# Fused attention and ELU feed-forward on one core: the largest magnitudes spread through PSUM instead of DRAM

## The chip, the cores and the metric

The kernel runs on one core of a Trainium2 chip. The core has a matrix engine (PE, with its weight loads shown apart as PEld), a vector engine (DVE), an activation engine (ACT), a general engine (POOL), and a sync engine whose queue (SP) issues all the kernel's DMA transfers, in order. SBUF is the on-chip memory with 128 partitions, PSUM the small memory that PE writes and DVE and ACT read, DRAM the memory outside. The metric is the device time of one execution in microseconds (us); lower is better.

## The reference, cut to what matters

```python
# q, k, v: (8 batches, 8 heads, 576 positions, 64), s: (8, 8, 576); all float32
scores = q @ k^T / 8, masked causally, plus min(-(cum_i - cum_j), 0)   # cum: running sum of max(s, 0)
attn   = softmax(scores)                    # row by row
x      = (attn @ v), heads side by side     # (4608 tokens, 512)
h      = x @ w_in                           # w_in (512, 2048)
g      = where(h > 0, h, exp(min(h, 0)) - 1)
out    = g @ w_out                          # w_out (2048, 512), float32
```

## The kernel before, in words

The attention runs by batch, by pair of heads (four pairs in a batch, `j`), and by blocks of 128 queries. The feed-forward part runs by chunks (`ch`, twelve of 384 tokens), and inside a chunk by 16 blocks of 128 hidden columns (`f`). For each `f`, PE makes the hidden product `h` (line 1312), ACT and DVE turn it into `gg` (lines 1276, 1321, 1330), and PE adds the projection to `o` (line 1349). Attention and feed-forward are interleaved. PE makes the scores `sc` (line 964), DVE adds the mask and takes the minimum (`p`, `mn`, line 967), ACT takes the exponential (line 972), POOL, ACT and DVE make halves of `p` (lines 1017, 1021, 1025), DMA transposes turn them (`T`, line 383), and PE weighs the values with them (`av`, line 1126).

Most products use two float16 halves of each operand, a high half and a low half, after scaling by a power of two. The scale comes from the largest magnitude of the operand, over all partitions. Chunk 0 is the exception: it runs in float32 (lines 1296 and 1341) while the scales of the weights aren't known yet. Attention of the first three batches' early blocks also runs in float32 and needs none.

The function `scales_of` finds such scales. It is called nine times: once for the two weight matrices (with three spans of columns), and once for each of eight groups of values. `peak` (line 574) has put one largest magnitude for each partition and each loaded piece into a column of `peaks`. `scales_of` reduces these to one number for each partition (`own`, line 593), stores them into DRAM (`aside`, 128 numbers of 4 bytes for each span), and loads the 128 numbers back into every partition (`every`). DVE then takes the largest in each partition and turns its exponent into a scale (lines 596, 598, 582). `split_unit` uses the weights' scales: it makes 32 high halves (line 402, 403) and 32 low halves on DVE (line 650) before chunk 1 can run. `group_values` loads the values of a group (`va`), takes their peaks and asks for their scale, 60 steps of priority ahead of their use.

The order of all instructions is set by a planner, `Plan.issue`. Each operation has a priority, a list of engines with assumed costs, and the buffers that it takes. The planner keeps a clock for each engine and always takes the operation that can start first, the priority deciding ties. For a transfer it assumes a lag until the data has landed: 5000 ns for the store to `aside`, 4500 ns for the load of `every`, 1800 ns for most others. Each engine then runs its list in the order found, and an instruction whose data isn't there holds up what stands behind it on the same engine. On SP this means that a load that waits holds up all later transfers. PSUM banks are buffers too: tag `a` (2 banks) and tag `av` (1 bank) serve scores, turned tiles and the weighing of values; tags `h` and `o0` to `o2` serve the feed-forward part, and scores when these are free.

Of the kernel before, what the change touches and what calls it, by code (L numbers as in the profile page):

```python
# [9 lines left out]
F32 = mybir.dt.float32  # L10
F32R = mybir.dt.float32r
U32 = mybir.dt.uint32
# [3 lines left out]
ALU = mybir.AluOpType  # L16

P = 128
# [6 lines left out]
SMALLEST = 2.0**-12  # L25
TOP, DOWN = 13, 22
# [55 lines left out]
class Plan:  # L82
# [87 lines left out]
    def issue(self):  # L170
# [3 lines left out]
        taken = dict.fromkeys(self.tags, 0)  # L174
# [15 lines left out]
        while pending:  # L190
            if free["PE"] > FILL_T:
                for o in [o for o in pending if o.filler]:
                    pending.remove(o)
                    for b in o.bufs:
                        b.users -= 1
                if not pending:
                    break
            best = None
            held = slots.get(self.signal, ())
            busy = free["PE"] > DYN_T or held and held[-1].users and not held[-1].others  # L200
            for o in pending:
                t = 0.0
                for b, k in o.new:
                    at = None
                    if taken[b.home] == k:
                        b.key, b.bufs = b.home, b.home_bufs
                        at = slot_free(b.key, b.bufs)
                    if b.others and (b.always or not busy):
                        for key, bufs, *rule in b.others:
                            if rule and not rule[0](taken[key]):  # L210
                                continue
                            other = slot_free(key, bufs)
                            if other is not None and (at is None or other < at):
# [26 lines left out]
            engine = self.ENGINE.get(engine, engine)  # L240
            if len(o.ways[n]) > 3:

                pipe = max(pipe, end) + o.ways[n][4] / RATE
                lag = pipe + o.ways[n][3] - end
            self.log.append((engine, start, end, o.prio))
            free[engine] = end
            for b, k in o.new:
                gone = skipped.setdefault(b.home, set())
                gone.add(k)
                while taken[b.home] in gone:  # L250
                    gone.remove(taken[b.home])
                    taken[b.home] += 1
                slots.setdefault(b.key, []).append(b)
            for b in o.bufs:
                b.until = max(b.until, end + lag)
                b.users -= 1
            pending.remove(o)
            for d in o.before:
                d.ready[engine] = max(d.ready.get(engine, 0.0), end + lag)
            for d in o.behind:  # L260
                d.ready[None] = max(d.ready.get(None, 0.0), start)
            for d in (*o.before, *o.behind):
                d.left -= 1
                if not d.left:
                    pending.append(d)
            at = len(block.instructions)
            trace()
            for i in block.instructions[at:]:
                if i.engine in last:
                    self.tc.add_manual_dep(  # L270
                        i, last[i.engine],
                        mybir.DependencyInfo(
                            mybir.DependencyClass.NoSync, mybir.DependencyReason.DATA
                        ),
                        reason="planned order",
                    )
                last[i.engine] = i.name
# [8 lines left out]
def pe4(n):  # L286

    return 4 * pe(n)
# [41 lines left out]
def kernel(  # L330
# [26 lines left out]
    D = vb.shape[4]  # L357
# [19 lines left out]
    def load(prio, dst, src, reads, writes, nbytes, late=(), lag=LAG):  # L377
        return op(prio, [("SP", SP_COST, lambda: nc.sync.dma_start(dst(), src()), lag, nbytes)],
                  reads, writes, late)
# [182 lines left out]
    A_GROUP = A_OUT + NF + 1  # L562
    peaks = plan.buf(const, [P, A_GROUP + len(groups) * (NP + 1)], F32, "peaks")

    scales = plan.buf(const, [P, 4 + 2 * len(groups)], F32, "scales")

    def scale_tiles():
        op(-8, [("Pool-M", 400.0, lambda: pool.memset(peaks.v, SMALLEST))], [], [peaks])
        op(-8, [("Pool-M", 60.0, lambda: pool.memset(scales.v, 1.0))], [], [scales])

    def peak(prio, n, src, reads, at, axis=mybir.AxisListType.X, aside=None, also=()):

# [8 lines left out]
    def power(out, src, top):  # L581
        dve.tensor_scalar(out, src, -1.0, float(top << 23), ALU.mult, ALU.add)

    def scales_of(prio, spans, dst):

        n = len(spans)
        own = plan.buf(sb, [P, n], F32, f"own_{dst}", tag=f"own{n}")
        aside = plan.buf(dram, [n, P], F32, f"aside_{dst}")
        every = plan.buf(sb, [P, n * P], F32, f"every_{dst}", tag=f"every{n}")

        def largest():
            for m, (at, k) in enumerate(spans):
                dve.tensor_reduce(own.v[:, m : m + 1], peaks.v[:, at : at + k], mybir.AxisListType.X, ALU.max)

        def exponents():
            dve.tensor_reduce(own.v, every.v.rearrange("p (n q) -> p n q", q=P), mybir.AxisListType.X, ALU.max)
            bits = own.v.bitcast(U32)
            dve.tensor_scalar(bits, bits, 23, 23, ALU.logical_shift_right, ALU.logical_shift_left)
            power(scales.v.bitcast(U32)[:, dst : dst + n], bits, 2 * 127 + TOP)

        used = [(peaks, m) for at, k in spans for m in range(at, at + k)]
        op(prio, [("DVE-SB", 60.0 + 70 * n, largest)], used, [own])
        load(prio, lambda: aside.v.rearrange("n p -> p n"), lambda: own.v, [own], [aside], P * n * 4, lag=5000.0)
        load(prio, lambda: every.v, lambda: aside.v.rearrange("n p -> (n p)").partition_broadcast(P),
             [aside], [every], P * P * n * 4, lag=4500.0)
        op(prio, [("DVE-SB", 500.0 + 130 * n, exponents)], [every], [own, (scales, dst)])

    def weight_scales():

# [213 lines left out]
    def group_values(u):  # L823

        at = groups.index((u.b, u.blocks[0] > 0))
        prio, first, col = u.prio - V_AHEAD, A_GROUP + at * (NP + 1), 4 + 2 * at
        home = w_parts[NG - 1] if at == 0 else w_all[(at - 1) % 2]
        va = plan.buf(sb, [P, NP, 2 * (NQ + 1), D], F32, f"va_{at}", tag=home.key[1])
        for j in range(NP):
            load(prio, lambda j=j: va.v[:, j], lambda j=j: vb[u.b, j, :, 1:], [], [(va, j)], P * 2 * (NQ + 1) * D * 4)  # L830
            peak(prio, 2 * (NQ + 1) * D, lambda j=j: va.v[:, j], [(va, j)], first + j, mybir.AxisListType.XY)
        scales_of(prio, [(first, NP + 1)], col)
        back = scales.v.bitcast(U32)
        op(prio, [("DVE-SB", 100.0, lambda: power(
            back[:, col + 1 : col + 2], back[:, col : col + 1], 2 * 127 - 15))], [(scales, col)], [(scales, col + 1)])
        return va, col
# [683 lines left out]
```

## Time and profile before

| what | value |
|---|---|
| median of 3 runs (lowest to highest) | 1129.79 us (1126.95 to 1129.88) |
| the profiled execution's own time | 1122.94 us |
| its span, first to last instruction | 1121.1 us |
| mean granted PE clock | 0.974 |
| DVE, ACT, POOL busy | 76%, 58%, 38% |
| DMA, mean rate | 140 GB/s |

The profile is of one execution, and its clock starts at the first instruction. A row of the order of time gives the start, the length (both in us), the engine, the source line, the operation, `out<-in`, and in brackets how long the engine had been idle before it, and what ended that idle time. SPq rows are the transfers' issues, not their landing. In a table by stretches, each engine has its busy time and its number of instructions; then follow the granted clock of PE (1.00 is full speed), the busy share of the DMA engines and their rate in GB/s. A row of waits gives the sum in us, the number of times and the longest.

### The profile page before, as it was taken

The numbers are of one execution on the slowest core, as the hardware profiler recorded it, in microseconds if no ns is written. First come the engines' busy times: TensorE is split into PE (matmuls) and PEld (weight loads), VectorE is DVE, ScalarE is ACT, GpSimd is POOL, SyncE is SP. The second block draws the span as 40 slices with busy tenths as digits, with TensorE's granted clock in tenths as the row PEclk, the third lists the DMA queues.
The fourth block names the chain that finished last, engine by engine and source line by source line (L and its number), as shares of the span: only waits on it lengthen the run. The fifth ranks groups of instructions, "written<-read, shape, count | busy, mean of one in ns | idle before, by whom it ended". The sixth has DMA issues, their size and how long they took to land. (4 is left out here: it accounts for less than half of the span.)

```text
span 1121.1 us, 19607 instructions
## 1 busy us (share of the span) xinstructions
PE 1036.3 (92%) x5970; PEld 614.3 (55%) x5970; DVE 856.2 (76%) x2218; ACT 646.5 (58%) x1525; POOL 422.4 (38%) x644
## 2 busy tenths in 40 slices
PE   8799998557999899988999989899989999999998
PEld 7576554234555455555555555455545656555554
DVE  7698895986888797897897798688879898643433
ACT  4687764535665565655665566456646565444433
POOL 5532453514564553553554454233243443100000
PEclk9899998978999999999999999899999999999999
DMA  6787895537567765676779667757857657310000
GB/s 174 195 238 224 223 230 126 176 52 121 142 170 193 118 151 144 156 160 162 150 177 163 139 144 197 114 122 175 172 99 189 143 123 164 70 57 1 29 1 28
DMA packets 307162, 157.24 MB, mean 140 GB/s; under 512 B 226649, under 2 KB 281841, under 8 KB 307057
## 3 DMA queue, kind: packets, MB, share of 16 engines
q1 hardware_dynamic: 307056, 156.00, 61.1%
q8 instruction: 47, 0.77, 0.3%
q14 instruction: 59, 0.48, 0.1%
HBM read 80.38 MB, written 19.32 MB: 89 GB/s over the span
## 5 line engine op out<-in xcount | busy, mean ns | idle before, releaser
L1312 PE MATMUL h<-xh,wp 128*128 128x384 f16 x1408 | 394.7, 331 | 16.1 <-DVE gg L1330 15.4
L1349 PE MATMUL o<-wp,gg 128*128 128x512 f16 x1584 | 389.7, 383 | 4.1 <-ACT gg L1325 3.4
L1312 PEld LDWEIGHTS <-wp 128*128 128x128 f16 x2112 | 200.1, 99 | 171.0 <-issue 34.0
L1349 PEld LDWEIGHTS <-gg 128*128 128x128 f16 x1584 | 146.6, 99 | 161.8 <-issue 7.1
L1312 PE MATMUL h<-xl,wp 128*128 128x384 f16 x704 | 232.5, 330 | 0.9 <-DVE xl L1265 0.9
L1276 ACT ACTIVATE g<-h,cs 128x384 f32<-128x384 f32 x176 | 102.0, 580 | 160.6 <-PE h L1312 158.6
L1025 DVE SCALAR_TENSOR_TENSOR p<-p,sm,p 128x512 f16<-128x512 f32 (+3 forms) x247 | 174.9, 728 | 10.1 <-ACT p L1021 7.5
L972 ACT ACTIVATE p<-p,mn 128x192 f32<-128x192 f32 (+1 forms) x232 | 144.0, 621 | 65.8 <-DVE mn L967 60.2
L1321 DVE SCALAR_TENSOR_TENSOR h<-g,cs,h 128x384 f32<-128x384 f32 x176 | 108.7, 618 | 92.8 <-ACT g L1283 91.6
L964 PE MATMUL sc<-kh,qs 128*128 128x192 f32 (+2 forms) x272 | 118.5, 438 | 34.4 <-DVE mn L967 33.5
L1017 POOL TENSOR_SCALAR p<-p,sm 128x512 f16<-128x512 f32 (+3 forms) x120 | 84.8, 712 | 159.1 <-DVE sm L978 50.4
L1325 ACT ACTIVATE gg<-h 128x384 f16<-128x384 f32 x162 | 78.9, 487 | 81.9 <-DVE h L1321 81.3
L967 DVE CUSTOM_DVE_ANT_0 p<-sc,maskw 128x192 f32<-128x192 f32 (+1 forms) x232 | 109.5, 481 | 16.1 <-PE sc L964 13.4
L1330 DVE SCALAR_TENSOR_TENSOR gg<-h,gg 128x384 f16<-128x384 f32 x176 | 96.9, 551 | 22.4 <-ACT gg L1325 18.7
L964 PEld LDWEIGHTS sc<-kh,qs 128*128 128x128 f32 x272 | 52.2, 192 | 63.7 <-DVE mn L967 21.7
L964 PE MATMUL sc<-k,q 128*128 128x192 f32 (+2 forms) x272 | 84.1, 314 | 2.0 <-DMA q<-qs 2.0
L1283 ACT ACTIVATE g<-g 128x384 f32<-128x384 f32 x140 | 73.1, 522 | 3.9
L411 POOL TENSOR_TENSOR k<-stk,kh 64x576 fp32r<-64x576 f32 x37 | 56.7, 1533 | 39.5 <-ACT kh L392 32.1
L1126 PE MATMUL av<-T,v 128*64 128x256 f16 (+5 forms) x896 | 63.0, 291 | 6.6 <-DMA T<-p 6.6
L1021 ACT ACTIVATE p<-p,sm 128x512 f16<-128x512 f32 (+3 forms) x98 | 55.9, 585 | 17.1 <-DVE sm L978 4.5
L1126 PEld LDWEIGHTS <-v 128*64 128x64 f16 x896 | 46.5, 111 | 31.7 <-issue 19.6
L411 POOL TENSOR_TENSOR qs<-stq,qs 64x512 fp32r<-64x512 f32 (+1 forms) x44 | 52.6, 1196 | 19.7 <-ACT qs L392 16.0
(173 smaller groups left out, 1388.3 us busy)
## 6 DMA issues: line engine op xcount, KB each, us to landing
stk<-in_kT_dram SPq DMA_DIRECT2D x64, 288.0 KB
va<-in_vb_dram SPq DMA_DIRECT2D x32, 320.0 KB
stq<-in_qT_dram SPq DMA_DIRECT2D x40, 256.0 KB
w_i<-in_w_in_dram SPq DMA_DIRECT2D x16, 512.0 KB
w_o<-in_w_out_dram SPq DMA_DIRECT2D x16, 512.0 KB
out_dram<-ost SPq DMA_DIRECT2D x32, 256.0 KB
x_dram<-x_None SPq DMA_DIRECT2D x20, 288.0 KB
q<-qs SPq DMA_DIRECT2D x40, 128.0 KB
```

The lines of the kernel that those rows point to most:

```text
L411: ("Pool", pool_2(n), lambda: pool.tensor_tensor(dst(), src(), hi(), ALU.subtract)),
L964: pe_.matmul(view(sc.v[:, :cw]), l, r, start=n == 0, stop=n == len(pairs) - 1)
L967: op(prio, [("DVE", 84 + dve_p(cw), lambda i=i, sc=sc: dve.tensor_tensor_reduce(pt.v[:, i * cw : (i + 1) * cw], sc.v[:, :cw], mv(i * cw, c ...
L972: op(prio, [("ACT", 480 + w / 1.2, lambda: act.activation(pt.v[:, :w], pt.v[:, :w], AF.Exp, bias=mn.v[:, n - 1 : n], scale=-1.0, accum_out ...
L1017: ("Pool", 160 + 1.04 * n, lambda part=part: pool.tensor_scalar(part(t16, 0), own(part), sm.v[:, r], 1.0, ALU.mult, ALU.mult)),
L1025: ("DVE-SB", dve_2(n), lambda part=part: dve.scalar_tensor_tensor(part(t16, 1), own(part), sm.v[:, r], part(t16, 0), ALU.mult, ALU.subtract)),
L1126: pe_.matmul(av.v[w.h * HB : (w.h + 1) * HB, dst], w.values.v[:, w.h, kb, v], part(w, kb, m), start=kb == 0 and m == 0 and v == 0, stop=kb ...
L1276: op(side, [("ACT", act_c(TC) + (0 if native else 90), lambda: act.activation(g.v[:, :TC], hp.v[:, :TC], AF.Exp, scale=1.0 if native else ...
L1312: pe_.matmul(hp.v[:, :TC], weight_part(f, 0, part)[1]()[:, c * P : (c + 1) * P], xx.v[:, c, :TC], start=(c == 0 and m == 0), stop=(c == NC ...
L1321: op(side, [("DVE", dve_p(TC), lambda: dve.scalar_tensor_tensor(hp.v[:, :TC], g.v[:, :TC], by(2 if sign[0] else 1), hp.v[:, :TC], ALU.mult ...
L1330: op(side, [("DVE", dve_p(TC), lambda: dve.scalar_tensor_tensor(gg.v[:, 1, :TC], hp.v[:, :TC], 2.0**-DOWN, gg.v[:, 0, :TC], ALU.mult, ALU. ...
L1349: pe_.matmul(acc[i].v, gg.v[:, g, tb], weight_part(f, 1, part)[1](), start=(f == 0 and m == 0), stop=(f == NF - 1 and m == 2),)
```

## The change

The store to `aside` and the load of `every` are gone. In their place, the per-partition maxima are written into the columns of a constant 128x128 tile (`tops`, its other columns filled once with the smallest magnitude). A product with the identity on PE turns it, so that row m of `flat` in PSUM holds the 128 maxima of span m. DVE takes the largest along each row, turns it into the scale, and multiplies it into the first n columns of the identity, which leaves the scales on a diagonal (`own`). A product with a 128x128 tile of ones gives every partition all n scales (`every`, now in PSUM), and DVE copies them to `scales`. `flat` and `every` take whichever bank of the tags `a` and `av` is free first; `any_bank` gives them no bank of their own, which is why the planner's test on `home_bufs` is added.

In `group_values`, the four loads of a group's values get priorities one step apart instead of the same one.

```diff
-                    if taken[b.home] == k:
+                    if b.home_bufs and taken[b.home] == k:
...
+    all_tops = [plan.buf(const, [P, P], F32, f"tops_{m}") for m in range(2)]
+    all_ones = plan.buf(const, [P, P], F32, "all_ones")
...
+    def any_bank(name):
+        return plan.buf(ps, [P, 512], F32, name, tag="any", bufs=0, others=[("a", N_A), ("av", N_AV)], always=True)
...
-        own = plan.buf(sb, [P, n], F32, f"own_{dst}", tag=f"own{n}")
-        aside = plan.buf(dram, [n, P], F32, f"aside_{dst}")
-        every = plan.buf(sb, [P, n * P], F32, f"every_{dst}", tag=f"every{n}")
+        tops = all_tops[n > 1]
+        flat, every = any_bank(f"flat_{dst}"), any_bank(f"every_{dst}")
+        own = plan.buf(sb, [P, 4], F32, f"own_{dst}", tag=f"own{n}")
...
         def exponents():
-            dve.tensor_reduce(own.v, every.v.rearrange("p (n q) -> p n q", q=P), mybir.AxisListType.X, ALU.max)
-            bits = own.v.bitcast(U32)
+            dve.tensor_reduce(own.v[:, 3:4], flat.v[:, :P], mybir.AxisListType.X, ALU.max)
+            bits = own.v.bitcast(U32)[:, 3:4]
             dve.tensor_scalar(bits, bits, 23, 23, ALU.logical_shift_right, ALU.logical_shift_left)
-            power(scales.v.bitcast(U32)[:, dst : dst + n], bits, 2 * 127 + TOP)
+            power(bits, bits, 2 * 127 + TOP)
+            dve.tensor_scalar(own.v[:, :n], ident[:, :n], own.v[:, 3:4], None, ALU.mult)
...
-        op(prio, [("DVE-SB", 60.0 + 70 * n, largest)], used, [own])
-        load(prio, lambda: aside.v.rearrange("n p -> p n"), lambda: own.v, [own], [aside], P * n * 4, lag=5000.0)
-        load(prio, lambda: every.v, lambda: aside.v.rearrange("n p -> (n p)").partition_broadcast(P),
-             [aside], [every], P * P * n * 4, lag=4500.0)
-        op(prio, [("DVE-SB", 500.0 + 130 * n, exponents)], [every], [own, (scales, dst)])
+        op(prio, [("DVE-SB", 60.0 + 70 * n, largest)], used, [tops])
+        op(prio, [("PE", pe4(P), lambda: pe_.matmul(flat.v[:, :P], tops.v, ident, start=True, stop=True))],
+           [tops], [flat])
+        op(prio, [("DVE", 600.0, exponents)], [flat], [own])
+        op(prio, [("PE", pe4(P), lambda: pe_.matmul(every.v[:, :n], all_ones.v, own.v[:, :n], start=True, stop=True))],
+           [all_ones, own], [every])
+        op(prio, [("DVE", 160.0, lambda: dve.tensor_copy(scales.v[:, dst : dst + n], every.v[:, :n]))],
+           [every], [(scales, dst)])
...
-            load(prio, lambda j=j: va.v[:, j], lambda j=j: vb[u.b, j, :, 1:], [], [(va, j)], P * 2 * (NQ + 1) * D * 4)
+            load(prio + j, lambda j=j: va.v[:, j], lambda j=j: vb[u.b, j, :, 1:], [], [(va, j)], P * 2 * (NQ + 1) * D * 4)
```

In the new program source lines after 573 are later by 5 to 13. Since the planner plans everything anew, the whole order shifts; two places are shown.

The first is SP's queue at the first of the nine calls, early in the float32 attention. `kl`, `ql` and `vs` are loads of keys, queries and values of the low blocks, `w_i` and `w_o` of weight blocks. Before:

```order
L378 DMA ql_3_350<-in_qT_dram 64x640
L378 DMA aside_355<-own_332 128x1
L378 DMA kl_3_345<-aux_dram 1x2x320
L378 DMA vs_90<-in_vb_dram 128x7x64
L378 DMA x_dram<-xl_0_385 128x320
L378 DMA w_i_413<-in_w_in_dram 128x4x256
L378 DMA every_437<-aside_355 128x128
L378 DMA x_0_440<-x_dram 128x320
```

And now:

```order
L378 DMA ql_3_355<-in_qT_dram 64x640
L378 DMA kl_3_350<-aux_dram 1x2x320
L378 DMA vs_90<-in_vb_dram 128x7x64
L378 DMA x_dram<-xl_0_391 128x320
L378 DMA w_i_421<-in_w_in_dram 128x4x256
L378 DMA x_0_444<-x_dram 128x320
```

Here only the two transfers are gone; what stood behind them keeps its order.

The second is DVE's queue at the call for the weights, near the end of chunk 0. `wp` are the halves of the weights, `gg_12` to `gg_15` the last blocks of chunk 0, `sc` scores of attention, `cs` a chunk's factors. Before, from the reduction of `every` on:

```order
L596 TENSOR_REDUCE own_2018<-every_2123 128x3
L598 TENSOR_SCALAR own_2018<-own_2018 128x3
L582 TENSOR_SCALAR scales<-own_2018 128x3
L1025 SCALAR_TENSOR_TENSOR p_3_2_0_0_2_2166<-p_87,sm_2_0_0_2092,p_3_2_0_0_2_2166 128x4x128
L967 ISA p_87,mn_2_1_0_2_2210<-sc_2_1_0_2_0_2194,maskw 128x448
L967 ISA mn_2_1_0_2_2210 128x1
L582 TENSOR_SCALAR scales<-scales 128x1
L650 SCALAR_TENSOR_TENSOR wp_2205<-wa_377,scales,wp_2205 128x512
L1302 SCALAR_TENSOR_TENSOR gg_14_2227<-h_14_2164,g_14_2202 128x384
```

And now, after the copy of `scales` and the factors `cs`:

```order
L663 SCALAR_TENSOR_TENSOR wp_2040<-wa_386,scales,wp_2040 128x512
L1153 TENSOR_SCALAR x_1_None_1905<-av_1_1_0_2043,scales 128x512
L663 SCALAR_TENSOR_TENSOR wp_2040<-wa_386,scales,wp_2040 128x512 x2
L1315 SCALAR_TENSOR_TENSOR gg_12_2109<-h_12_2022,g_12_2096 128x384
L663 SCALAR_TENSOR_TENSOR wp_2040<-wa_386,scales,wp_2040 128x512 x5
L1315 SCALAR_TENSOR_TENSOR gg_13_2140<-h_13_2111,g_13_2127 128x384
L663 SCALAR_TENSOR_TENSOR wp_2092<-wa_930,scales,wp_2092 128x512 x6
L1315 SCALAR_TENSOR_TENSOR gg_14_2170<-h_14_2146,g_14_2163 128x384
L663 SCALAR_TENSOR_TENSOR wp_2092<-wa_930,scales,wp_2092 128x512 x2
```

Before, one of the 32 low halves stood ahead of `gg_15`, the last block of chunk 0, and the others behind it; now 17 of the 32 stand ahead of it, and the attention of head pair 2 of batch 3 has moved behind chunk 0 in their place.

On PE, the turning product and the spreading product of a call stand apart: one row lies between them at the call for the weights, 6 to 68 rows at the others.

More of the change, by code (lines that the diff above doesn't have):

```diff
@@ L569, in scale_tiles @@
         op(-8, [("Pool-M", 60.0, lambda: pool.memset(scales.v, 1.0))], [], [scales])
+        for tops in all_tops:
+            op(-8, [("Pool-M", 150.0, lambda tops=tops: pool.memset(tops.v, SMALLEST))], [], [tops])
+        op(-8, [("Pool-M", 150.0, lambda: pool.memset(all_ones.v, 1.0))], [], [all_ones])
     def peak(prio, n, src, reads, at, axis=mybir.AxisListType.X, aside=None, also=()):
@@ L591, in largest @@
         def largest():
             for m, (at, k) in enumerate(spans):
-                dve.tensor_reduce(own.v[:, m : m + 1], peaks.v[:, at : at + k], mybir.AxisListType.X, ALU.max)
+                dve.tensor_reduce(tops.v[:, m : m + 1], peaks.v[:, at : at + k], mybir.AxisListType.X, ALU.max)
         def exponents():
-            dve.tensor_reduce(own.v, every.v.rearrange("p (n q) -> p n q", q=P), mybir.AxisListType.X, ALU.max)
-            bits = own.v.bitcast(U32)
+            dve.tensor_reduce(own.v[:, 3:4], flat.v[:, :P], mybir.AxisListType.X, ALU.max)
```

## The prediction

> **What bounds the kernel now.** I read the page's busy times first, then PE's waits, then the order of time around each call of `scales_of`.
>
> ```profile
> PE 1036.3 (92%) x5970; PEld 614.3 (55%) x5970; DVE 856.2 (76%) x2218; ACT 646.5 (58%) x1525; POOL 422.4 (38%) x644
> ```
>
> PE is busy for 92%, so the time is PE's work plus PE's idle time, 1121.1 - 1036.3 = 84.8 us. What ends the idle time:
>
> ```profile
> PE sc L964 <- DVE mn L967: 33.5, 12, 16.7
> PE h L1312 <- DVE gg L1330: 15.4, 13, 4.9
> PE av L1126 <- DMA T<-p: 6.6, 2, 5.1
> PE avl L775 <- DVE tl L418: 4.6, 2, 4.4
> ```
>
> A few long waits make most of it. They are not spread evenly: they stand a few us behind the store to `aside`. The first call, in order of time:
>
> ```profile
> 23.25 0.54 SPq L378 DMA_DIRECT2D aside<-own  x1
> 24.58 0.40 SPq L378 DMA_DIRECT2D vs<-in_vb_dram  x1
> 30.39 0.46 PE L964 MATMUL sc<-kl,ql 128*128 128x128 f32 x2 [2.54 <-DMA kl<-aux_dram]
> 32.90 0.32 SPq L378 DMA_DIRECT2D every<-aside  x1
> 33.93 0.62 DVE L574 TENSOR_REDUCE peaks<-vs 128x1 f32<-128x448 f32 x1 [7.93 <-DMA vs<-in_vb_dram]
> 35.21 1.12 PE L775 MATMUL avl<-tl,vs 128*128 128x64 f32 x4 [4.37 <-DVE tl L418]
> ```
>
> `every` is issued 9.65 us behind `aside`, where the planner assumed 5. And `vs`, issued 1.3 us behind `aside`, lands 9.3 us later; DVE idles 7.93 us for it, and PE 2.54 + 4.37 = 6.91 us. The last call, and below it the same kind of load at a place without `aside`, and the DMA rate in six us of the last call:
>
> ```profile
> 808.63 0.46 SPq L378 DMA_DIRECT2D aside<-own  x1
> 809.93 0.36 SPq L378 DMA_DIRECT2D stk<-in_kT_dram  x1
> 819.12 0.34 SPq L378 DMA_DIRECT2D every<-aside  x1
> 822.21 0.46 DVE L394 TENSOR_SCALAR kh<-stk 128x576 fp32r<-128x576 f32 x1 [5.20 <-DMA stk<-in_kT_dram]
> 823.15 0.40 PE L964 MATMUL sc<-kh,qs 128*128 128x288 f32 x1 [2.69 <-DVE mn L967]
> ...
> 158.88 0.36 SPq L378 DMA_DIRECT2D stk<-in_kT_dram  x1
> 161.75 0.68 ACT L392 ACTIVATE kh<-stk 128x576 fp32r<-128x576 f32 x1 [0.39 <-DMA stk<-in_kT_dram]
> ...
> 815.00:821.00 6.00, 4.63 (x25) 2.33 (x22) 2.01 (x7) 2.09 (x5) 0.00 (x0) 1.00 0.36 23
> ```
>
> The load of keys takes 12.3 us beside the store and 2.9 us alone, and DMA moves 23 GB/s there, against the mean of 140 in the table above. So the store costs twice: it slows transfers in flight, and `every` holds SP's queue until it has landed. The second shows in SP's waits, and the nine pairs in the tile's row:
>
> ```profile
> SPq L378 <- ACT ost L1380: 77.6, 10, 54.2
> ...
> SPq L378 <- DMA aside<-own: 25.8, 6, 6.8
> ...
> L378 SPq DMA_DIRECT2D aside<-own x9: 327/455/797, 23.3 to 808.6; - x9
> ```
>
> I can't part slowed transfers from the held queue, but the change takes both away.
>
> **The change, part by part.**
>
> *A, the first call* (23 to 41 us): PE's 6.91 us of idle time, plus what follows a long gap: half the granted clock. First and last of nine such stretches of 4 to 7 us (the columns end with clock, DMA share, GB/s):
>
> ```profile
> 35.00:40.00 5.00, 4.79 (x17) 4.05 (x18) 3.21 (x16) 4.27 (x15) 1.52 (x4) 0.57 0.80 240
> ...
> 824.00:828.00 4.00, 4.00 (x14) 1.65 (x13) 3.83 (x9) 1.48 (x4) 2.07 (x2) 0.57 1.05 181
> ```
>
> Each costs busy time x (1 - clock): 4.79 x 0.43 = 2.1 us and 4.00 x 0.43 = 1.7 us. A is 6.9 + 2.1 = 9.0 us. In the new order the same loads follow without the pair, and `vs` should land in some 3 us, as the quiet load did; about 1 us of DVE's wait may stay. I take -8; ends -5 and -9.
>
> The Trainium skill, "TensorE: Matmul & The Clock Gate", section "What's actually happening", says that the clock halves after an idle window of about 3.4 us. By it the gaps of 2.7 to 2.9 us below would cost no clock, and the sum would be some 5 us smaller; but the trace has 0.57 right behind a gap of 2.69, so I count them.
>
> *B, the weights' call and the two calls after it* (169 to 272 us). Here DVE is the bound:
>
> ```profile
> 184.78 0.50 PE L964 MATMUL sc<-kh,qs 128*128 128x192 f32 x1 [4.19 <-DVE mn L967]
> 209.81 0.34 PE L1312 MATMUL h<-xh,wp 128*128 128x384 f16 x1 [4.94 <-DVE gg L1330]
> 234.99 0.50 PE L964 MATMUL sc<-kh,qs 128*128 128x192 f32 x1 [16.70 <-DVE mn L967]
> 244.66 0.32 PE L1312 MATMUL h<-xh,wp 128*128 128x384 f16 x1 [2.40 <-DVE gg L1330]
> 265.67 0.61 PE L964 MATMUL sc<-kh,qs 128*128 128x288 f32 x1 [5.64 <-DVE mn L967]
> ...
> 169.00:272.00 103.00, 68.65 (x300) 37.29 (x299) 76.81 (x180) 45.66 (x105) 34.75 (x44) 0.83 0.54 116
> ...
> L1025 DVE SCALAR_TENSOR_TENSOR p<-p,sm,p 128x512 f16<-128x512 f32 x127 | 108.7, 871 | 4.4 <-ACT p L1021 2.9 <-POOL p L1017 1.0
> ...
> L650 DVE SCALAR_TENSOR_TENSOR wp<-wa,scales,wp 128x512 f16<-128x512 f32 x32 | 25.6, 864 | 0.0
> ...
> 166.97 2.74 PE L1296 MATMUL h<-x,wa 128*128 128x384 f32 x8
> 169.55 2.74 PE L1341 MATMUL o<-wa,gg 128*128 128x512 f32 x6
> ```
>
> PE idles 33.9 us in these five gaps, while DVE does 76.8 us of work in 103. The 32 low halves (25.6 us) come in one block after chunk 0, when PE has little left to do. In the new order 17 of them, not 1, stand ahead of the last block of chunk 0, whose remaining nine float32 steps (four hidden, five projections) cover 9 x 2.74 = 24.7 us on PE. That moves 16 x 0.864 = 13.8 us of DVE work under PE's work. Against it, DVE work of the attention of head pair 2 moves out from there to behind chunk 0; by the order of before it is about seven mask operations and four halves; at no more than the 0.87 us of the largest halves (line 1025) that is under 9.6 us, and I estimate 7 to 8. Net some 6 us. The gaps of 4.19 and 5.64 stand behind an `aside` (173 and 250 us) and go, 9.8 us, and their two cold stretches with them, about 5 us. That would be 21. But DVE is busy here, and what a gap gives, the next DVE queue partly takes back: the 16.70 gap will shrink, not vanish. I take -15; ends 0 (DVE takes all back) and -30.
>
> *C, the last five calls* (372 to 828 us). Gaps within 16 us behind their `aside`, beside 823.15 above:
>
> ```profile
> 383.18 0.98 PE L1349 MATMUL o<-wp,gg 128*128 128x512 f16 x3 [2.91 <-ACT gg L1325]
> 511.46 0.33 PE L964 MATMUL sc<-k,q 128*128 128x192 f32 x1 [1.13 <-DMA q<-qs]
> 519.82 1.46 PE L1126 MATMUL av<-T,v 128*64 128x512 f16 x13 [1.44 <-DMA T<-p]
> 614.72 0.33 PE L964 MATMUL sc_None<-k2s,q2s 128*128 128x128 f32 x1 [2.73 <-DMA q2s<-qs_None]
> 723.50 2.83 PE L1126 MATMUL av<-T,v 128*64 128x512 f16 x14 [5.14 <-DMA T<-p]
> ```
>
> 2.91 + 1.13 + 1.44 + 2.73 + 5.14 + 2.69 = 16.0 us, and four cold stretches of 1.7 to 2.7, together 7.8: 23.8 us. PE is the bound on both sides of each, so this counts in full if the transfers land in time. The DMA transposes `T` have little slack of their own; a fifth may stay. I take -19; ends -9 and -24.
>
> *D, what is added.* PE gets 18 products in float32. The nearest row:
>
> ```profile
> L964 PE MATMUL sc<-kl,ql 128*128 128x128 f32 x22 | 4.6, 290 | 3.9 <-DMA kl<-aux_dram 2.8 <-DMA ql<-in_qT_dram 0.6 <-issue 0.4
> ```
>
> These 22 records are 11 products, 0.42 us each. The nine turning products have that size, the nine spreading ones have 1 or 3 columns and cost less: between 9 x 0.42 = 3.8 and 18 x 0.42 = 7.6; I take 5. Both wait for DVE, and what is queued behind them on PE waits too. At the weights' call one hidden product lies between the two, elsewhere 6 to 68 rows, so mostly the wait is covered; 0.2 us for each of nine calls, +2. DVE loses nothing much: for each call two short operations more, and the largest is taken over the same 128 numbers. SP loses 18 issues of about 0.4 us. The loads of values set one step apart change no queue that I can see: in the new SP order seven of the eight groups stand as four in a row, before five did. Zero, covered by the 60 steps of lead; without that cover a load of a quarter group is late, about 3 us once, as the quiet load above. D is +7; ends +4 and +10.
>
> Sum: -8 - 15 - 19 + 7 = -35, from 1122.9 to 1088 in the profiled execution. The median of the runs shown is 6.9 us above that execution, so I forecast a median of 1129.8 - 35 = 1095.
>
> **The rivals.**
>
> *Only partly.* DVE takes all of B back, the transposes keep half of C: -8 + 0 - 11 + 7 = -12, so 1118. For it: DVE is 76% busy, and the five gaps of B all end at DVE. Against it: in C the waits end at transfers.
>
> *Hidden anyway.* The gaps come from loads that are late in any case, and the pair costs the queue nothing; then only D is left, +7: 1137. For it: SP also waits 77.6 us in ten places for `ost`, so waiting is normal for it. Against it: the same load takes 2.9 us alone and 12.3 beside the store, and the rate falls to 23 GB/s. The Trainium skill, "DMA: Bandwidth & Descriptors", section "Anatomy of one DMA — SWDGE (gpsimd) path", puts the fixed cost of a transfer at about 2 us; by it the pair would take some 4 us, less than the planner allows for, nothing would be late, and 1137 would come out. The trace shows 9.65 and 10.5 us from `aside` to `every`, so I give this little.
>
> *Banks, the other sign.* `flat` holds one of three banks (two of `a`, one of `av`) until DVE has read it. In the new DVE order 32, 23 and 28 rows lie between filling `tops` and reading `flat` at the calls 4, 5 and 6 from the start; at 856.2 / 2218 = 0.39 us a row that is up to 12.5, 9 and 11 us with a bank less, and scores queue behind it on PE. Were PE to idle for all of it, +32, against -35: about no change, 1127. It decides for slower when the gains are also only partly there (-12): then 1150. Against it: 6 to 68 rows of other PE work lie between, and scores may use five other banks.
>
> **How the numbers follow.** My forecast has 0.58, for 1080 to 1110. All gaps and more go (A -9, B -30, C -24, D +4: 1071): 0.09. Only partly: 0.21, of which 0.03 within the bound. Hidden anyway: 0.05, slower. Banks: 0.07, of which 0.03 no change and 0.04 slower. About 0.3%, 3.4 us, is what a measurement of this kernel can tell from no change. So faster 0.85, same 0.06, slower 0.09. The range goes from 1073, near all gaps gone, to 1124, which takes in the partly case with its spread.
>
> **What the new profile would show.** A: no PE gap over 2 us between 23 and 41 us, and DMA rates that don't fall. B: PE idle time from the weights' call to the sixth block of chunk 1 down from 34 to about 20 us. C: no PE gap over 2 us within 16 us behind a turning product. D: each turning and spreading product under 0.45 us, with little idle ahead. I am wrong if gaps of the same length stand at the same calls with transfers still late, if the float16 stretch after chunk 0 has more idle time than before, or if PE waits for DVE at `flat` or `every`.

## The result, and the profile after

| kernel | median, us (lowest to highest) | ratio to before, 95% interval | profiled execution: own time, span, clock |
|---|---|---|---|
| before | 1128.37 (1125.62 to 1129.88), 4 runs | 1 | 1122.94, 1121.1, 0.974 |
| changed | 1088.22 (1085.21 to 1090.53), 4 runs | 0.9645 [0.9611, 0.968] | 1086.86, 1085.1, 0.981 |

The changed kernel is faster by 3.6%. The profiled executions differ by 36.1 us, the forecast by steps was 35; for the median it was 1095. The sum came out, but A was put too high and C too low, and the reason for term B was partly wrong; that these errors cancel is luck. Below, the page's row of busy times after, and what ends PE's idle time:

```profile
PE 1029.2 (95%) x6007; PEld 617.8 (57%) x6007; DVE 858.9 (79%) x2214; ACT 646.8 (60%) x1530; POOL 442.8 (41%) x672
...
PE h L1325 <- DVE gg L1343: 15.7, 19, 4.9
PE h L1325 <- DVE mn L980: 9.9, 1, 9.9
PE flat L613 <- DVE tops L602: 5.0, 1, 5.0
PE sc L977 <- DMA ql<-in_qT_dram: 2.4, 1, 2.4
...
PE sc L977 <- DVE mn L980: 1.8, 5, 0.9
```

PE idles 1085.1 - 1029.2 = 55.9 us, before 84.8. The 33.5 us of scores waiting for DVE (12 times) have shrunk to 1.8 us (5 times), and the waits for turned tiles `T` are gone. New are the 9.9 us in which a hidden product waits for the same work of DVE, and the wait of `flat` for `tops`. For the three stretches of the prediction, in stretches of equal length, first before (the middle one stands in the prediction), then after:

```profile
23.00:41.00 18.00, 11.09 (x57) 9.08 (x55) 8.14 (x31) 7.45 (x27) 4.38 (x12) 0.81 0.61 144
372.00:828.00 456.00, 425.67 (x2562) 246.65 (x2561) 375.52 (x992) 272.58 (x637) 196.19 (x276) 0.98 0.73 152
```

```profile
23.00:41.00 18.00, 13.73 (x71) 11.24 (x71) 12.69 (x46) 11.30 (x37) 6.52 (x14) 0.81 0.85 205
169.00:272.00 103.00, 77.91 (x393) 46.33 (x392) 92.14 (x212) 56.03 (x131) 48.88 (x56) 0.85 0.52 136
372.00:828.00 456.00, 445.83 (x2763) 262.01 (x2763) 395.50 (x1037) 286.09 (x666) 230.59 (x332) 1.00 0.71 162
```

The length less PE's busy time is its idle time: 6.9 us before and 4.3 after in the first stretch, 34.4 and 25.1 in the second, 30.3 and 10.2 in the third. More work falls into each stretch after, so the comparison is one of rates and good to a few us.

At the first call `vs` now starts DVE 3.1 us after its issue (before 9.3), but one gap stays, and a stretch of half clock around it:

```profile
23.72 0.41 SPq L378 DMA_DIRECT2D vs<-in_vb_dram  x1
26.80 0.62 DVE L579 TENSOR_REDUCE peaks<-vs 128x1 f32<-128x448 f32 x1 [1.03 <-DMA vs<-in_vb_dram]
32.48 0.60 SPq L378 DMA_DIRECT2D ql<-in_qT_dram  x1
36.23 2.05 PE L977 MATMUL sc<-kl,ql 128*128 128x128 f32 x6 [2.40 <-DMA ql<-in_qT_dram]
...
33.00:40.00 7.00, 4.36 (x14) 3.41 (x14) 4.50 (x14) 3.80 (x13) 2.86 (x5) 0.54 0.95 204
33.60:33.80 0.20, 0.20 (x2) 0.00 (x0) 0.20 (x3) 0.20 (x1) 0.20 (x1) 0.50 1.16 159
```

`ql` is issued late, into a stretch in which the DMA engines are 0.95 busy. The gap of 2.40 us ends at 36.23, so it begins at 33.83; the clock is at 0.50 already at 33.60, so this gap isn't what halved it. The last call has nothing left to see: the load behind it goes out at once, PE is busy for all of the 6 us, and DMA moves 169 GB/s where it moved 23.

```profile
771.48 0.38 PE L613 MATMUL flat<-ident,tops 128*128 128x128 f32 x2
772.49 0.37 SPq L378 DMA_DIRECT2D stk<-in_kT_dram  x1
...
771.00:777.00 6.00, 6.00 (x56) 4.33 (x54) 5.70 (x20) 3.96 (x9) 4.53 (x7) 1.00 0.70 169
```

Behind the weights' call PE's long gaps are these; all but the third (POOL) end at DVE. The last rows are the two products' groups.

```profile
192.93 0.33 PE L1098 MATMUL av_None<-pc_None,vs_None 128*128 128x128 f32 x1 [1.31 <-DVE pc_None L1048]
202.15 0.77 PE L613 MATMUL flat<-ident,tops 128*128 128x128 f32 x2 [5.04 <-DVE tops L602]
209.13 0.47 PE L977 MATMUL sc_None<-khs_None,qs_None 128*128 128x128 f32 x1 [3.12 <-POOL qs_None L411]
220.46 0.48 PE L1325 MATMUL h<-xh,wp 128*128 128x384 f16 x1 [9.92 <-DVE mn L980]
231.04 0.48 PE L1325 MATMUL h<-xh,wp 128*128 128x384 f16 x1 [4.92 <-DVE gg L1343]
...
L613 PE MATMUL flat<-ident,tops 128*128 128x128 f32 x18 | 3.8, 298 | 5.0 <-DVE tops L602 5.0
...
L616 PE MATMUL every<-own,all_ones 128*128 128x1 f32 (+1 forms) x18 | 2.9, 231 | 0.0
```

### The profile page after: what moved, and what is told of

The parts are those of the page before. It is cut to its first block, busy times and chain, and to the rows that moved or that the text cites. A ratio compares the mean times of both kernels' runs of the same rounds, so it can differ in the third digit from the quotient of the medians.

```text
span 1085.1 us, 19692 instructions
## 1 busy us (share of the span) xinstructions
PE 1029.2 (95%) x6007; PEld 617.8 (57%) x6007; DVE 858.9 (79%) x2214; ACT 646.8 (60%) x1530; POOL 442.8 (41%) x672
## 4 chain that ended last, share of the span: by engine, by line
PE 67%; DVE 16%; DMA 7%; issue 4%; POOL 4%; ACT 2%; SPq 0%; DVEq 0%; POOLq 0%; ACTq 0%
PE o L1362 24%; PE h L1325 24%; PE sc L977 7%; PE av L1139 4%; DVE p L1038 3%; PE h L1309 3%; PE o L1354 2%; DVE xl L1278 1%; DMA w_i<-in_w_in_dram 1%; DVE gg L1343 1%; DMA stq<-in_qT_dram 1%; DVE h L1334 1%; DVE wp L663 1%; DVE p L980 1%; PE avl L788 1%
## 5 line engine op out<-in xcount | busy, mean ns | idle before, releaser
L1038 DVE SCALAR_TENSOR_TENSOR p<-p,sm,p 128x512 f16<-128x512 f32 (+3 forms) x242 | 170.7, 726 | 3.0 <-ACT p L1034 1.8
L1030 POOL TENSOR_SCALAR p<-p,sm 128x64 f16<-128x64 f32 (+3 forms) x125 | 85.4, 690 | 136.5 <-DVE sm L991 67.3
L1338 ACT ACTIVATE gg<-h 128x384 f16<-128x384 f32 x156 | 76.0, 487 | 82.4 <-DVE h L1334 81.6
L1296 ACT ACTIVATE g<-g 128x384 f32<-128x384 f32 x147 | 76.6, 521 | 4.0
L411 POOL TENSOR_TENSOR k<-stk,kh 64x576 fp32r<-64x576 f32 x41 | 62.9, 1535 | 15.8 <-ACT kh L392 13.7
L402 POOL TENSOR_SCALAR xh<-xc,cs 128x384 f16<-128x384 f32 x28 | 21.7, 784 | 103.8 <-PE h L1325 99.2
L1034 ACT ACTIVATE p<-p,sm 128x512 f16<-128x512 f32 (+3 forms) x93 | 53.1, 590 | 14.0 <-DVE sm L991 7.0
```

Source lines behind the costliest of these rows:

```text
L1030: ("Pool", 160 + 1.04 * n, lambda part=part: pool.tensor_scalar(part(t16, 0), own(part), sm.v[:, r], 1.0, ALU.mult, ALU.mult)),
L1038: ("DVE-SB", dve_2(n), lambda part=part: dve.scalar_tensor_tensor(part(t16, 1), own(part), sm.v[:, r], part(t16, 0), ALU.mult, ALU.subtract)),
L1296: act.activation(g.v[:, :TC], g.v[:, :TC], AF.Relu, bias=1.0, scale=-1.0)
```

## The experiments

What stayed open was why the pair cost so much: the store slows other transfers, or the load that waits for it holds SP's queue, or the gain is that of the new order. Each ratio is to the kernel before, run on the same chip; not all groups of runs had the same chip, so between groups ratios compare better than microseconds.

**The pair put back, unused, into the new order.** `store_alone` adds one line to the reduction (`largest`). The planner is told of no cost, so the order of PE, DVE, ACT and POOL stays that of the changed kernel row by row.

```diff
                 dve.tensor_reduce(tops.v[:, m : m + 1], peaks.v[:, at : at + k], ...)
+            nc.sync.dma_start(aside.v.rearrange("n p -> p n"), tops.v[:, :n])
```

> The changed kernel (1088 us), with the old store of the maxima (128 numbers of 4 bytes for each span, to DRAM) issued again at each of the nine calls, right behind the reduction that makes them. Nobody reads what it stores, and the order of all other instructions stays as it is. Theory 1, slowed transfers: the store itself slows the transfers behind it. Then loads issued right behind it land after 6 to 12 us instead of 2 to 5, and most of parts A and C comes back: 1105 to 1115 us. Rival 2, held queue: only the load that waited for the store did harm, by holding SP's queue. Then nothing comes back: 1088 to 1092. Rival 3, the order: the new order of instructions brought the gain, and the transfers never stood in the way: 1088.

Measured: 1129.92 us, 0.9976 [0.9944, 1.0008]. The store alone takes back all of the gain, more than the 1105 to 1115 that I expected. Its row of busy times, the first call, and six us of it, and behind them the same six us of the changed kernel:

```profile
PE 1041.2 (92%) x6007; PEld 619.4 (55%) x6007; DVE 859.9 (76%) x2214; ACT 647.8 (57%) x1530; POOL 438.6 (39%) x672
...
21.39 0.35 SPq L604 DMA_DIRECT2D aside<-tops  x1
23.97 0.40 SPq L378 DMA_DIRECT2D vs<-in_vb_dram  x1
33.75 0.76 PE L979 MATMUL sc<-kl,ql 128*128 128x128 f32 x2 [5.77 <-DMA ql<-in_qT_dram]
34.07 0.62 DVE L579 TENSOR_REDUCE peaks<-vs 128x1 f32<-128x448 f32 x1 [7.98 <-DMA vs<-in_vb_dram]
...
26.00:32.00 6.00, 1.98 (x11) 1.29 (x9) 0.09 (x1) 0.88 (x4) 1.50 (x4) 0.83 0.60 41
```

```profile
26.00:32.00 6.00, 4.44 (x25) 3.59 (x24) 3.60 (x17) 3.39 (x12) 1.86 (x6) 1.00 0.90 242
```

Nobody reads what was stored, and yet `vs` takes 10.1 us (23.97 to 34.07) instead of 3.1, and DMA moves 41 GB/s instead of 242 while its engines are 0.60 busy: they are occupied and move little. It isn't the pieces that occupy them. In the microsecond from 22 to 23, the engines' records have 144 packets of 4 bytes, 9 ns each at most; from 23 to 25 there follow packets of 1280 bytes that take up to 6.5 us (in the changed kernel none of that size takes over 0.8 us from 20 to 32 us). The share counts a packet's whole time where it begins:

```profile
22.00:23.00 1.00, 0.18 (x1) 0.18 (x2) 0.97 (x3) 0.76 (x2) 0.08 (x1) 1.00 0.08 1
23.00:24.00 1.00, 1.00 (x9) 0.98 (x10) 0.66 (x4) 0.73 (x3) 0.00 (x0) 1.00 1.90 90
```

`store_and_load` adds the load as well, from `aside[0]` into all partitions, at the place of the copy of `scales`.

> The changed kernel with both old transfers issued again and unused: the store of 4-byte pieces at each call, and the load of 128 numbers into all partitions, which waits for it on SP's queue, at the place of the copy of the scales. The order of all other instructions stays as it is. Theory 1, slowed transfers: as with the store alone, with at most 5 us more: 1105 to 1118. Rival 2, held queue: all of the loss comes with this one and not with the store alone: 1105 to 1120 here, 1088 to 1092 there. Rival 3, the order: 1088 to 1091, since nobody waits for either transfer.

Measured: 1136.22 us, 1.0037 [1.0006, 1.0068]. The load does hold SP's queue, as long in all as it did before (25.8 us):

```profile
SPq L623 <- DMA aside<-tops: 26.3, 4, 8.9
```

That is worth some 6 us more than the store alone (0.0061 of the time, at the edge of what can be told: the two intervals overlap by 0.0002; 1118 was the most I expected), against 37 us of the store by the ratios to before, 42 by the times. So the first theory stands, and the held queue is a small part.

`row_and_load` stores one row for each span from one partition, `nc.sync.dma_start(aside.v, tops.v[:n])`, and keeps the load.

> As with store and load, but the store takes one contiguous row of 512 bytes for each span from one partition instead of 128 pieces of 4 bytes. A trip through DRAM of the same kind and a waiting load are there; the small pieces are not. Theory 1, slowed transfers by the small pieces: the store lands in 2 to 4 us, nothing else is slowed, and the time is 1088 to 1093. Rival 2, held queue, whatever the store's shape: the load still waits on SP for some us at each call, and about a third to a half of the loss of the pair comes back: 1095 to 1105. Rival 3, the order: 1088 to 1091.

Measured: 1090.29 us, 0.9632 [0.9589, 0.9675]: a trip through DRAM, load included, costs nothing that can be told from the changed kernel, and SP's waits have no row for its store. What is slow is the store in 128 pieces.

**What it is about the pieces.** The same unused store in four other forms, the loads as they are:

```diff
-aside: [n, 128] numbers in DRAM, 4-byte pieces side by side         # store_alone
+aside: [n, 128, 128], the same pieces 512 bytes apart               # store_apart
+aside: [n, 128, 16], the same pieces 64 bytes apart                 # store_64
+aside: [n, 128, 128], 128 pieces of 512 bytes (all of tops)         # store_512
+to an SBUF tile, 4-byte pieces, partition to partition              # store_in_sbuf
```

> The changed kernel with the unused store again at each of the nine calls (store alone gave 1130 us), but its 4-byte pieces land 512 bytes apart in DRAM instead of side by side. Theory a, the same place: 128 pieces written into the same 512 bytes of DRAM get into each other's way; apart, they don't: 1088 to 1093. Theory b, the small piece: each piece under 512 bytes is slow by itself wherever it lands: 1120 to 1135. Theory c, the number of pieces: 128 of them are too many of whatever size: 1120 to 1135.

> The same unused store with 128 pieces of 512 bytes (the whole tile of maxima, one row from each partition, also at the weights' call). Theory a, the same place: each piece has a place of its own, 1088 to 1093. Theory b, the small piece: 1088 to 1095, since no piece is small, and 64 KB more at each call is what any load here moves. Theory c, the number of pieces: 1120 to 1135.

> The same unused store with 4-byte pieces, but to another tile in SBUF, partition to partition, instead of to DRAM. Theory a, the same place in DRAM: 1088 to 1093. Theory b, the small piece: as slow as the store alone if reading small pieces or their handling is slow, 1120 to 1135; 1088 to 1093 if it is their writing into DRAM. Theory c, the number of pieces: 1120 to 1135.

> The unused store once more, its 4-byte pieces 64 bytes apart in DRAM, so eight of them share 512 bytes (side by side gave 1130 us, 512 bytes apart 1091). If the conflict is between pieces within the same 512 bytes: part of the loss comes back, 1095 to 1120, since eight pieces wait for each other instead of 128. If it is between pieces within the same 64 bytes or less: 1089 to 1093. If the span of addresses of the whole store decides and not the single step: 1110 to 1130.

| run | us | ratio to before | `vs` at the first call, issue to use, us |
|---|---|---|---|
| store_alone | 1129.92 | 0.9976 [0.9944, 1.0008] | 10.1 |
| store_apart | 1091.33 | 0.9665 [0.9636, 0.9694] | 3.5 |
| store_64 | 1090.37 | 0.9699 [0.9667, 0.9732] | 3.2 |
| store_512 | 1093.13 | 0.9679 [0.965, 0.9709] | 3.6 |
| store_in_sbuf | 1093.09 | 0.9675 [0.9643, 0.9707] | 3.6 |

The rows behind the table's second line (`store_apart`):

```profile
24.43 0.40 SPq L378 DMA_DIRECT2D vs<-in_vb_dram  x1
27.93 0.62 DVE L579 TENSOR_REDUCE peaks<-vs 128x1 f32<-128x448 f32 x1 [1.90 <-DMA vs<-in_vb_dram]
```

(At the weights' call `store_in_sbuf` has 128 pieces of 12 bytes, since its three columns lie side by side.) Not the number of pieces, nor their size, nor DRAM as such: of the forms tried, only pieces of 4 bytes side by side in DRAM are slow, and 64 bytes apart is far enough. Theory a stands. In `store_64` the engines' records have the same 144 packets of 4 bytes from 22 to 23 us, again 9 ns each at most, but behind them, up to 25 us, no packet takes over 0.45 us: the loss lies in what the pieces do to the transfers behind them. The step between 4 and 64 bytes at which it begins wasn't tried, and what happens inside the memory no row shows. The Trainium skill, "DMA: Bandwidth & Descriptors", section "Specifications", states that a transfer under 512 bytes is read, changed and written back. By itself that can't be the cause here, since 4-byte pieces 64 bytes apart are under 512 too and took 1090 us: it is the neighbourhood of the pieces, not their size alone.

**Another queue.** `store_other_queue` issues the slow store with `nc.scalar.dma_start`, from ACT's queue, behind the reduction of `flat`.

> The unused store with its pieces side by side, as in the store alone (1130 us), but issued from ACT's queue, behind DVE's reduction of flat, instead of SP's. Theory q, the line: the loads are late because they stand behind the slow pieces in SP's own line of transfers; on another engine's queue they pass: 1089 to 1096, a few us for what ACT waits and issues. Theory e, the shared engines: the pieces hold the 16 DMA engines, or the memory, for all queues: 1115 to 1135.

Measured: 1125.27 us, 0.9999 [0.9971, 1.0028]. The first rows are the first call, the last two the weights':

```profile
21.21 0.34 ACTq L607 DMA_DIRECT2D aside<-tops  x1
24.49 0.41 SPq L378 DMA_DIRECT2D vs<-in_vb_dram  x1
33.92 0.62 DVE L579 TENSOR_REDUCE peaks<-vs 128x1 f32<-128x448 f32 x1 [2.12 <-DMA vs<-in_vb_dram]
...
170.10 0.38 ACTq L607 DMA_DIRECT2D aside<-tops  x1
...
182.86 1.46 PE L1141 MATMUL av<-T,v 128*64 128x512 f16 x6 [8.43 <-DMA T<-p]
```

`vs` still takes 9.4 us, from a queue in which the store doesn't stand, as theory e has it. So the pieces hold what the queues share; another queue is no way out. The Trainium skill, same page, section "Issuing engines are not separate DMA queues", says that transfers run on the same 16 engines whoever issues them; this run agrees.

**The order.** `before_row` is the kernel before, its planned order kept (one short operation on DVE more for each call), with the store as one row. The row is a constant, so the true maxima are left out and the scales are constants.

```diff
             dve.tensor_reduce(own.v[:, m : m + 1], ...)
+            dve.memset(row[0:1, : n * P], 8.0)
-        load(prio, lambda: aside.v.rearrange("n p -> p n"), lambda: own.v, [own], [aside], ...)
+        load(prio, lambda: aside.v.rearrange("(o n) p -> o (n p)", o=1), lambda: row[0:1, : n * P], [own], [aside], ...)
```

> The kernel before, its order kept, with the store of 128 pieces of 4 bytes replaced by a store of one row of 512 bytes for each span (a constant, written by one short operation more on DVE at each call; the true maxima are left out, so the scales are constants). Store and load through DRAM stay. It parts the transfers from the new order. Theory 1, the pieces alone: with them gone the time falls by all that the change brought, and by the products it lacks: 1082 to 1094. Rival, the order has its share: the gain that my part B put on the moved halves (some 6 us of its 15) and the rest of the new order are missing, while A, C and the gaps of B behind the store go: 1094 to 1105. Rival 2, the order has more than half of it: 1105 to 1120.

Measured: 1086.04 us, 0.9617 [0.9588, 0.9645]. The old order, without the pieces, is as fast as the changed kernel. With one row, `every` is issued 2.7 us behind `aside` at the first call (26.36 and 23.63 us), before the change 9.65. The stretch of part B and its long gaps:

```profile
169.00:272.00 103.00, 77.70 (x400) 43.62 (x399) 89.62 (x212) 55.24 (x125) 40.69 (x52) 0.90 0.56 132
...
202.20 0.48 PE L1314 MATMUL h<-xh,wp 128*128 128x384 f16 x1 [4.93 <-DVE gg L1332]
227.37 0.50 PE L966 MATMUL sc<-kh,qs 128*128 128x192 f32 x1 [16.83 <-DVE mn L969]
236.30 0.32 PE L1314 MATMUL h<-xh,wp 128*128 128x384 f16 x1 [2.05 <-DVE gg L1332]
```

PE idles 25.3 us here, in the changed kernel 25.1. The gap of 16.83 stands as before (16.70); the two gaps behind a store (4.19 and 5.64) are gone. The half clock costs 3.8 us in this stretch (each us by busy time x (1 - clock)), in the changed kernel 6.5. So the moved low halves, with the rest of the new order, show no gain for PE here.

**The loads a step apart.** `no_step` takes back `prio + j` for `prio`.

> The changed kernel with the four loads of a group's values at the same priority again, as before the change. My prediction put this edit at zero: 1085 to 1091 us. Rival: the step sets the loads apart in time, and without it some loads of keys or queries stand behind a row of four large loads: about 3 us for each place at which PE waits, 1091 to 1097. Second rival: the new plan shifts instructions elsewhere and gives a difference of either sign, with no mechanism at the loads: 1080 to 1096.

Measured: 1087.56 us, 0.9607 [0.9571, 0.9643], against 0.9645 [0.9611, 0.968] with the step. By the traces, PE, DVE, ACT, POOL and SP carry out the same operations on the same tiles (buffer numbers left out) in the same order with the step and without it. So that edit does nothing that shows, and the two ratios show how far one order differs from itself between two groups of runs: 0.0038.

**A better version.** What is left behind the weights' call ends at DVE, which is busy for 92.14 of 103 us there, POOL for 48.88. These two kernels make some of the weights' low halves on POOL:

```diff
+        if f in LOW_POOL:       # (2, 5, 8, 11) or (1, 3, 5, 7, 9, 11), both matrices
+            pool.tensor_scalar(spare, value(), scales.v[:, col], 1.0, ALU.mult, ALU.mult)
+            pool.tensor_tensor(low_v(), spare, high_v(), ALU.subtract)
```

> The changed kernel with 8 of the 32 low halves of the weights (blocks 2, 5, 8 and 11, both matrices) made on POOL instead of DVE, in two steps through a scratch tile (a scaled copy, then a subtraction). From the changed kernel's rows, a step of 320 columns takes 0.53 and 0.79 us there, so one low half of 512 some 2.1 us, 17 us for the eight; DVE loses 8 x 0.86 = 6.9 us. Theory, DVE still bounds the stretch behind the weights' call, where PE idles 24 us: idle falls by up to 7 us, 1080 to 1084. Rival, DVE's place in the line is taken by POOL, which is late with the queries and the halves of p: 1088 to 1098. Rival 2, the first hidden products wait for scores' masks in DVE's order and not for DVE's amount of work: 1086 to 1090.

> The same with 12 of the 32 low halves on POOL (blocks 1, 3, 5, 7, 9 and 11): 25 us of POOL's time, 10.4 us less on DVE. Theory, DVE bounds the stretch: 1078 to 1083, below the kernel with eight. Rival, POOL becomes late, and more so than with eight: 1090 to 1102. Rival 2, DVE's order decides: 1086 to 1090.

Measured: with eight 1089.68 us, 0.969 [0.9663, 0.9718], not the 1080 to 1084 of the theory but where both rivals had put it; with twelve 1074.6 us, 0.9566 [0.9534, 0.9599], below the 1078 to 1083 of the theory and faster than the changed kernel, whose interval begins at 0.9611, and than the kernel with eight on the same chip (1071.4 to 1081.15 us against 1085.59 to 1090.34). The stretch with eight, then with twelve, then two groups and the two longest gaps of the latter:

```profile
169.00:272.00 103.00, 84.94 (x414) 47.43 (x413) 81.69 (x191) 58.94 (x127) 51.96 (x63) 0.88 0.49 127
```

```profile
169.00:272.00 103.00, 93.58 (x463) 52.43 (x462) 82.61 (x190) 62.83 (x137) 60.44 (x70) 0.94 0.45 121
...
L668 POOL TENSOR_SCALAR spare<-wa,scales x12: 688/786/1151, 172.0 to 198.6; 128x512 f32<-128x512 f32 x12
L669 POOL TENSOR_TENSOR wp<-spare,wp x12: 1157/1338/1638, 172.7 to 199.4; 128x512 f16<-128x512 f32 x12
...
202.41 0.53 PE L988 MATMUL sc<-kh,qs 128*128 128x192 f32 x1 [3.92 <-POOL qs L413]
...
268.74 0.37 PE L1336 MATMUL h<-xh,wp 128*128 128x384 f16 x1 [2.36 <-DVE gg L1354]
```

PE's idle time there falls from 25.1 to 18.1 us with eight, the 7 us expected, and to 9.4 with twelve, by more than the 10.4 us of work taken from DVE. With eight the whole time didn't follow: every such edit gives a new plan, and what the stretch gained was lost outside it (gaps of 2.56 and 2.74 us at 747 and 908 us among others); over the whole span PE idles 57.4 us, in the changed kernel 55.9. The long gaps of its stretch (4.33, 5.22 and 3.29 us) end at DVE and not at POOL, so the rival of a late POOL isn't borne out. That DVE bounds the stretch is supported by both kernels; that twelve are better than eight as such is not shown, since the rest of the plan changed too: DVE is busy for 81.69 us in the stretch with eight and 82.61 with twelve.

## Why the prediction was right, and where its steps were not

*The transfers.* That the store slows what is in flight was right, and is now shown: it carries the whole gain. That it costs twice was wrong in weight: the held queue is worth some 6 us, the slow pieces 37 to 42. The prediction could not part the two and said so.

*A, -8.* The idle time fell by 2.6 us, and the half clock cost the same as before (4.36 x 0.46 = 2.0 us against 2.1). A gave 2.6, below its end of 5. `vs` came in 3.1 us as forecast; the mis-sized step was to count the next loads as free. They run into busy DMA engines (0.95): the next `vs`, issued at 30.21 us, starts DVE 7.2 us later. Of the signs that the prediction named, "no gap over 2 us" didn't come true, with one of 2.40; and the half clock begins ahead of that gap, not behind it as the prediction has it.

*B, -15.* Idle time fell from 34.4 to 25.1, 9.3 us, and over those stretches in which the clock was down the loss fell from 9.8 to 6.5 us (each us by busy time x (1 - clock)): 12.6 in all, near the forecast, but not for all of its reasons. The two gaps behind a store and their cold stretches went, as stated. The moved halves, "net some 6 us", gave nothing: the old order has the same idle time and less half clock. They were counted as gain because they moved under PE's work; that DVE's queue, busy for 92.14 of 103 us, simply takes the gain back, as the prediction feared, is likely but not parted from the rest of the new order. The group of low halves is also no cheaper than before (25.6 us, 864 ns each):

```profile
L663 DVE SCALAR_TENSOR_TENSOR wp<-wa,scales,wp 128x512 f16<-128x512 f32 x32 | 27.4, 914 | 0.0
```

The 16.70 gap hardly shrank either: its place is now held by 5.04 (`flat` waits for `tops`, which stands behind seven low halves and four `peaks` on DVE) and 9.92.

*C, -19.* Idle time fell by 20.1 us and the 7.8 us of half clock are gone, no stretch behind 234 us shows it: 28, beyond the end of 24. I counted the 16.0 us of six gaps near the stores; the small ones around them went too. The sign "no PE gap over 2 us within 16 us behind a turning product" came true there: the longest gap behind 372 us has 1.59 us. In `before_row` PE idles 13.4 us there, so most of C needs the pieces gone and not the new order. And the fifth held back for the transposes `T` was not needed: none of PE's waits after is for `T`.

*D, +7.* The products take 3.8 + 2.9 = 6.7 us (5 forecast), 298 and 231 ns for a record, two records for a product. Eight of the nine turning products take 0.38 or 0.39 us; the one at 202.15 us, at half clock, takes 0.77, more than the 0.45 of the prediction's sign. PE's one wait for DVE at them, 5.04 us, is what the prediction named as a sign that it is wrong, and no term had it. It probably stands where PE would else have waited for DVE a little later, since `before_row` has the same idle time without it. The step of one between the loads was put at zero, and is.

*What had no term.* Outside the three stretches (41 to 169, 272 to 372, 828 to 1084) PE idled 5.5 us before and 11.7 after, 6 us of small gaps, and a new stretch of half clock at 84 us costs 1.7. A new plan shifts these by itself; the range held it, the sum did not. At the two ends of the span (up to 23 and behind 1084 us) PE idles 3 us less. With A to D this is -2.6 - 12.6 - 28 + 6.7 + 6 + 1.7 - 3 = -32 of the measured -36. The rest stays open: hidden products and projections take 3 ns less each in their groups (331 to 328, 383 to 380 ns), but the half clock, counted above, lengthens these groups too, so this can't simply be added.

*The rivals.* "Hidden anyway" is refuted by the store alone; the 2 us that the prediction quotes there are, as the name of the section says, for another path than SP's queue. "Only partly" is what A and B did in part, and C made up for it. "Banks": PE waited once at `flat`, and for DVE's reduction ahead of it, not for a bank.

## What to carry to other kernels

A small store can be the dearest transfer of a kernel: find it by loads that take 10 us behind it and 3 elsewhere while DMA's rate falls, and put one back alone into the new order before believing what a new order brings. Here a trip through DRAM in one row was as fast as no trip at all; but the row held nothing that was needed, so what it costs to bring 128 maxima into one row isn't in these runs, and reading back pieces 64 bytes apart wasn't tried. Work moved off a gap helps only if the engine that ends the gap has room where it goes; giving twelve pieces of it to an engine that is busy for half of the time did help, giving it eight did not.

## What the runs showed of the hardware that I had not expected

- 128 pieces of 4 bytes written side by side into DRAM slow the loads behind them (`vs` takes 9.3 to 11.3 us, the keys at the last call 12.3, without such a store some 3), whether they are issued from SP's queue or ACT's; 64 bytes apart they cost next to nothing (1090 against 1130 us), and in SBUF too. Three times the pieces don't take three times as long: in the kernel before, the weights' call stores 384 pieces, three spans, and its `every` is issued 10.0 us behind `aside` (183.11 and 173.09 us), at the first call with 128 pieces 9.65.
- The busy share of the DMA engines stays at 0.60 while they move 41 GB/s: it is no measure of what they bring, since a packet that takes long counts as busy all the while.
- The granted clock fell to 0.59 in the changed kernel from 84 to 88 us, where the longest gap ahead was 0.88 us, though PE had been busy for only 2.39 of the four us before. So a single long gap isn't needed for the half clock:

```profile
80.00:84.00 4.00, 2.39 (x12) 1.31 (x10) 2.76 (x10) 2.75 (x9) 0.54 (x3) 1.00 0.74 210
84.00:88.00 4.00, 3.96 (x16) 3.27 (x17) 3.08 (x10) 2.37 (x8) 1.20 (x4) 0.59 0.85 219
```
